# A Fourier layer with a maxout FFN on one core: stores issued by GpSimd, half as many moves for stage Q, half as many loads for the second half of x

## The chip, the cores and the metric

One core of one Trainium2 chip runs the whole program in one launch. The metric is the device time of the launch in microseconds (us). The kernel before took 2103.49 us, the median of 3 runs (2101.82 to 2107.21).

## What is computed

Eight sequences of 3072 tokens with 256 channels go through a Fourier layer: a real FFT along the tokens, a complex 256x256 product with a bias, a soft threshold at 0.01, and the inverse FFT. The 24576 tokens that come out go through a maxout FFN.

```python
x: (8, 3072, 256)   w_r, w_i: (256, 256)   w1, w2, w3: (256, 768)   w_out: (768, 256)

X = np.fft.rfft(x, axis=1)
Yr = Xr @ w_r - Xi @ w_i + b_r
Yi = Xr @ w_i + Xi @ w_r + b_i
Y = soft(Yr) + 1j * soft(Yi)          # soft(v) = sign(v) * max(|v| - 0.01, 0)
y = np.fft.irfft(Y, n=3072, axis=1)   # (8, 3072, 256), as 24576 tokens
h = np.maximum(np.maximum(y @ w1, y @ w2), y @ w3)
out = h @ w_out                       # (24576, 256)
```

## The kernel before

The FFT of length 3072 is done as 96 x 32 by matrix products on TensorE. Most products are of numbers split into two halves of 16 bits (a high and a low part, `split` and `split_later`: ScalarE writes the high part, VectorE the low one) and take three matmuls (`mm3`, lines L175 to L177).

The Fourier layer has these stages for each of the 8 batches, named by the tiles they make:

- **Stage A**, 8 chunks per batch: `load_x` brings a chunk of x (4 of 32 columns), `sum_x` adds and subtracts its two halves on VectorE (from batch 3 on, chunk number `q >= HALF_X`), `split_x` splits it, `stage_a` multiplies by the DFT over 96 into PSUM tile `pa`. ScalarE evicts `pa` to `aq` (L580), and four DMAs per chunk store `aq` to DRAM as `a_d` (L583; in earlier batches one, L596). `load_m` and `largest_m` read the same chunk of x once more (`xm`) for the largest magnitude.
- **Stage B**, 12 steps per batch: `load_a` brings two groups of rows of `a_d` into a tile `ab`, `split_a` splits them in place (ScalarE L635, VectorE L638), and four DMAs on SyncE's queue move the halves across partitions (`ab<-ab`, L643). `stage_b` multiplies by the DFT over 32 into `px` (L732, sixteen matmuls of 64 columns); the results are split again as `tt`.
- **Stage W**, 12 steps: products with the complex weights into `py` (`stage_w1`, `stage_w2`). ScalarE copies the first part to `cs` (L819), VectorE forms `u` from `py` and `cs` (L829), adds the bias and clamps (`soft_threshold`, L777 and L778). `finish_w` splits `u` into `vb` (ScalarE L169, VectorE L170), and eight DMAs on SyncE's queue move it across partitions (`vb<-vb`, L853). Step 11 of each batch is of another kind (`plain`): it has no moves, and GpSimd makes small copies for it (L760 to L769).
- **Stage Q**, once for two steps: `stage_q` begins the inverse transform, `vb` times `qt` into two tiles `pz` (L892); ScalarE evicts to `zs` (L898), and DMAs store `z_d` (L900).
- **Inverse**, 8 chunks per batch: `load_z` brings a chunk of `z_d` as `zq`, `split_z` splits it, `inverse` multiplies into `pi`, split as `yh` and `yl` (ScalarE L169).

The FFN runs all the time from batch 0 on: `up` makes three products per slot into `pu` and the maximum of them (ScalarE copies the first as `c`, L985; VectorE takes the maxima, L988 and L991, the last is `h`, split as `hh`), `down` adds up six slots in `pd`, and ScalarE evicts `pd` to `o` (L1020) three times per chunk, each followed by a store of 128 KB to `out` (L1021).

**Order.** A batch has 48 slots: 8 chunks, each with 6 parts of the FFN's width. Into these slots a list of `events` puts the stages of the later batches: while the FFN of batch b runs, the stages B, W and Q of batch b+1 run at one step per 2.8 slots, and stage A of batch b+2 at one chunk per 5.6 slots. So every batch's stages lie beside an earlier batch's FFN, up to batch 7. The framework then orders each engine's instructions. Each engine issues its own DMAs in its own order: while an engine issues a DMA, what is queued behind on it stands. SyncE (SP) has all loads and all moves; ScalarE (ACT) has the stores of `a`, `z` and `out`; GpSimd (POOL) has a few instructions of step 11 and two loads at the beginning. PSUM has 8 banks: three for `pu`, two for `pd`, and three in turn for `pa`, `px`, `py`, `pz` and `pi` (tag `ff`). Of the buffers that come round in turn, `raw` (tiles `ab` and `vb`) has 8, `aq` and `zs` 2, `o` 3.

Of the kernel before, what the change touches and what calls it, by code (L numbers as in the profile page):

```python
# [9 lines left out]
F32 = mybir.dt.float32  # L10
# [15 lines left out]
def dft_tables():  # L26

    n, n1n, n2n = 3072, 96, 32
    n1, n2, tp = np.arange(n1n), np.arange(n2n), 2 * np.pi
    fa, ga = np.zeros((n1n, 96)), np.zeros((96, n2n, n1n))
    for m in range(94):  # L40
        k1, c = 1 + m // 2, m % 2
        ph = tp * ((k1 * n1) % n1n) / n1n
        fa[:, m] = np.cos(ph) if c == 0 else -np.sin(ph)
        ph = tp * ((k1 * (32 * n1[None, :] + n2[:, None])) % n) / n
        ga[m] = (2.0 / n) * (np.cos(ph) if c == 0 else -np.sin(ph))
    alt = (-1.0) ** n1
    fa[:, 94], ga[94] = 1.0, 1.0 / n
    fa[:, 95], ga[95] = alt, alt[None, :] / n
    sg = np.where(n2 >= 16, -1.0, 1.0)

    def forward(k1):
        ang = tp * ((n2[:, None] * (k1 + 96 * n2[None, :])) % n) / n
        co, si = np.cos(ang), np.sin(ang)
        b = np.zeros((2, 32, 2, 32))
        b[0, :, 0], b[1, :, 0] = co, si
        b[0, :, 1], b[1, :, 1] = -si * sg, co * sg
        return b.reshape(64, 64)

    ang = tp * ((n2[:, None] * n2[None, :]) % 32) / 32
    co, si = np.cos(ang), np.sin(ang)  # L60
    q = np.zeros((2, 32, 2, 32))
    q[0, :, 0], q[1, :, 0] = co, -si * sg[:, None]
    q[0, :, 1], q[1, :, 1] = si, co * sg[:, None]
    bs, qs = np.zeros((2, 32, 2, 32)), np.zeros((2, 32, 2, 32))
    alt = (-1.0) ** n2
    bs[0, :, 0, 0], bs[0, :, 1, 0] = 1.0, alt
    qs[0, 0, 0, :], qs[1, 0, 0, :] = 1.0, alt
    for f in range(1, 32):
        c, k = (0, 96 * f) if f < 16 else (1, 48 + 96 * (f - 16))
        ph = tp * ((k * n2) % n) / n  # L70
        bs[c, :, 0, f], bs[c, :, 1, f] = np.cos(ph), -np.sin(ph)
        qs[0, f, c, :], qs[1, f, c, :] = 2 * np.cos(ph), -2 * np.sin(ph)
    z = np.zeros((64, 64))
    q, bs, qs = (v.reshape(64, 64) for v in (q, bs, qs))
    order = np.arange(128).reshape(2, 2, 32).transpose(1, 0, 2).ravel()
    blocks = [forward(k1) for k1 in range(1, 48)] + [bs]
    mb = [np.block([[blocks[i], z], [z, blocks[i + 1]]])[:, order] for i in range(0, 48, 2)]
    mq = [np.block([[u, z], [z, v]])[order] for u, v in ((q, q), (q, qs))]
    even, odd = (np.pad(fa[0:48, np.arange(96) % 4 // 2 == i], ((0, 16), (0, 16))) for i in (1, 0))
    tiled = np.block([[q, even], [q, odd]])  # L80

    def halves(v, scale):
        v = v * 2.0**scale
        hi = v.astype(np.float16)
        return np.ascontiguousarray(np.stack([hi, (v - hi).astype(np.float16)], 1))

    ga = ga[np.arange(96).reshape(24, 2, 2).transpose(1, 0, 2).ravel()]
    return (
        fa.astype(np.float32),
        halves(ga, SG),  # L90
        halves(np.stack([np.concatenate([v, v]) for v in blocks], 1), SB),
        np.ascontiguousarray(np.stack(mq + mb + [tiled], 1)).astype(np.float32),
        np.eye(128, dtype=np.float32),
    )
# [3 lines left out]
def fourier_maxout_kernel(  # L98
    ctx: ExitStack, tc: tile.TileContext, x, w_r, w_i, b_r, b_i, w1, w2, w3, w_out, fa, ga, mb, mq, ident, out
):  # L100
    nc = tc.nc
    NB, S, D = x.shape
    FF = w1.shape[1]
    P = 128
    N1, N2 = 96, 32
    KD = D // P
    NF = FF // P
    NQ = 4
# [9 lines left out]
    fft = ctx.enter_context(tc.tile_pool(name="fft", bufs=2))  # L118
# [4 lines left out]
    st = {}  # L123
# [87 lines left out]
    def raw_tile(name):  # L211
        return ffn.tile([P, 1536], F32, name=name, tag="raw", bufs=8)
# [257 lines left out]
    def load_x(q):  # L470
        b, q4 = divmod(q, NCH)
        xv = x[b].rearrange("(n1 n2) d -> n1 n2 d", n2=N2)[:, q4 * NQ:(q4 + 1) * NQ, :]
        with tc.issue_after(st["ld"].ins) if q >= EARLY else nullcontext():
            if 2 <= q < NCH or NCH + 2 <= q < EARLY:
                xq = raw_tile("xr")[0:N1, 0:NQ * D]
            else:
                xq = fft.tile([P, NQ * D], F32, name="xq", bufs=2)
                if q >= HALF_X:
                    second = [
                        fft.tile([P, 2, D], F32, name="x2", tag=tag, bufs=3) for tag in ("vl", "vh")  # L480
                    ]
                    xn = xq.rearrange("p (n d) -> p n d", n=NQ)
                    for r, n in ((0, 64), (64, 48)):
                        nc.sync.dma_start(out=xn[r:r + n], in_=xv[0:n])
                    for i, t in enumerate(second):
                        for r, n in ((0, 48), (48, 64)):
                            nc.sync.dma_start(out=t[r:r + n], in_=xv[96 - n:96, 2 * i:2 * i + 2])
                    st["x", q] = xq, second
                    return
                xq = xq[0:N1]  # L490
            nc.sync.dma_start(out=xq.rearrange("p (n d) -> p n d", n=NQ), in_=xv)
            pairs = [xq[:, i * 2 * D:(i + 1) * 2 * D] for i in range(2)]
        st["x", q] = pairs
# [29 lines left out]
        )  # L523

    def sum_x(q):
        xq, second = st.pop(("x", q))
        with in_turn():
            for i, t in enumerate(second):
                half = xq[0:112, i * 512:i * 512 + 512]
                nc.vector.scalar_tensor_tensor(  # L530
                    out=half, in0=t[0:112].rearrange("p n d -> p (n d)"), scalar=sign[0:112], in1=half,
                    op0=ALU.mult, op1=ALU.add,
                )
        st["x", q] = xq
# [28 lines left out]
    def stage_a(q):  # L563
        b, q4 = divmod(q, NCH)
        if q >= HALF_X:
            xt = st.pop(("xs", q))
            pa = [ff_tile("pa") for _ in range(2)]
            aq = fft.tile([P, NQ * D], F32, name="aq", bufs=2)
            for t, i in ((0, 0), (0, 1), (1, 0)):
                for r in range(2):  # L570
                    rows = slice(64 * r, 64 * r + 48)
                    for h in range(2):
                        st["mm"] = nc.tensor.matmul(
                            pa[r][64 * h:64 * h + 64], ft[rows, t], xt[rows, i, h],
                            start=t == i, stop=t == 1,
                        )
            av = batch(b, "a").rearrange("(k e c) n d -> e k c (n d)", e=2, c=2)
            for r in range(2):
                o = aq[:, 512 * r:512 * r + 512]
                nc.scalar.activation(out=o, in_=pa[r], func=AF.Copy, scale=1.0 / (X_SCALE * F_SCALE))  # L580
                for h in range(2):
                    n = q4 * NQ * D + h * 512
                    nc.scalar.dma_start(out=av[1 - r, :, :, n:n + 512], in_=o[64 * h:64 * h + 48])  # L583
            return
        aq = first_quads[q] if q < EARLY else quad_tile("aq")
        for i, xp in enumerate(st.pop(("xs", q))):
          with tc.issue_after(st["gate"]) if EARLY <= q < NATIVE else nullcontext():
# [5 lines left out]
            nc.scalar.activation(  # L593
                out=aq[:, i * 512:i * 512 + 512], in_=pa[0:96], func=AF.Copy
            )
        (nc.scalar if b else nc.gpsimd).dma_start(  # L596
            out=batch(b, "a")[:, q4 * NQ:(q4 + 1) * NQ, :], in_=aq.rearrange("p (n d) -> p n d", n=NQ)
        )
        if NCH <= q < HALF_X and q4 == NCH - 1:
# [119 lines left out]
    def stage_b(k):  # L719
# [5 lines left out]
        if plain(k):  # L725
            pv = px.rearrange("p (h j c q m) -> p h c j q m", h=KD, j=2, c=2, q=2)
        else:
            pv = px.rearrange("p (h c j q m) -> p h c j q m", h=KD, c=2, j=2, q=2)
        for g in range(4):
            for h in range(KD):  # L730
                for i in range(2):
# [105 lines left out]
    def finish_w(k):  # L837
# [3 lines left out]
        if b:  # L841
# [4 lines left out]
            split_later(v[:, 0], v[:, 1], u, st[b, "sv"][0])  # L846

            def move():
                for q in range(2):
                    for j in range(2):  # L850
                        for c in range(2):
                            row = 64 * q + 32 * c
                            nc.sync.dma_start(  # L853
                                out=moved[row:row + 32, kb % 2, :, j],
                                in_=v[64 * j + 32 * q:64 * j + 32 * q + 32, :, c],
                            )

            if not plain(k):
                later(move)
# [6 lines left out]
    def stage_q(k):  # L866
# [17 lines left out]
        elif kb % 2 == 1 or kb == NJP - 2:  # L884
# [11 lines left out]
            for q in range(2):  # L896
                zs = fft.tile([P, 2, D], F32, name="zs")
                nc.scalar.activation(out=zs[:, 0:n], in_=pz[q], func=AF.Copy, scale=st[b, "sv"][1])  # L898
                zv = z_rows(b, q).rearrange("(g j) p d -> (j p) g d", j=2)
                nc.scalar.dma_start(out=zv[:, kb + 1 - n:kb + 1], in_=zs[:, 0:n])  # L900
        if kb == NJP - 1:
            low, add = st["lim", "u"]
            e = exponent_of(st.pop((b, "u")), "u", 23, 0xFF, low)
# [97 lines left out]
    def down(b, c, f, hh):  # L1001
# [10 lines left out]
        if f == NF - 1:  # L1012
            for t in range(3):
# [4 lines left out]
                    )  # L1018
                else:
                    nc.scalar.activation(out=o, in_=pd[t], func=AF.Copy, scale=st[b, "su"][1])  # L1020
                (nc.sync if end and t < 2 else nc.scalar).dma_start(out=out_v[b, c, t], in_=o)  # L1021

    nc.sync.dma_start(out=fr, in_=fa)
    split(fh, fl, fr)
# [188 lines left out]
```

## Time and profile before

| | |
|---|---|
| median of 3 runs | 2103.49 us |
| the profiled execution | 2100.16 us, of which the span 2098.3 us |
| TensorE (PE), busy | 2014.0 us, 96% |
| weight loads (PEld) | 1378.7 us, 66% |
| VectorE (DVE) | 1469.5 us, 70% |
| ScalarE (ACT) | 1034.8 us, 49% |
| GpSimd (POOL) | 21.6 us, 1% |
| mean granted clock of TensorE | 0.991 |

Busy time counts computing instructions alone; the time in which an engine issues DMAs is not in it, and the views show it apart (ACTq, SPq). The span is the time from the first to the last instruction of the profiled execution. Weight loads overlap the matmuls. The granted clock is what the throttle gave, as a share of full speed (1.2 and 2.4 GHz are its two levels, 0.5 and 1 here).

### The profile page before, as it was taken

How to read it: one execution, taken by the hardware profiler on the slowest of the kernel's cores; microseconds unless marked ns; L12 is line 12 of the kernel's file. 1: busy time of each engine (PE TensorE's matmuls, PEld its weight loads, DVE VectorE, ACT ScalarE, POOL GpSimd, SP SyncE). 2: the span in 40 equal slices, each digit the busy share in tenths (PEclk: the TensorE clock that was granted, in tenths of full speed). 3: DMA queues.
4: the chain of work that ended last, by engine and by line, in shares of the span. 5: the costliest groups of instructions: out<-in, count | busy, mean ns of one | idle time of the engine just before them, and what ended most of it. 6: DMA issues, size and time to landing. Idle time of an engine off the chain costs nothing.

```text
span 2098.3 us, 42001 instructions
## 1 busy us (share of the span) xinstructions
PE 2014.0 (96%) x16335; PEld 1378.7 (66%) x16335; DVE 1469.5 (70%) x2809; ACT 1034.8 (49%) x2060; POOL 21.6 (1%) x75
## 2 busy tenths in 40 slices
PE   9989999999899999999999999999999999999999
PEld 5656666666566666666656666666666677766666
DVE  3778887787767877678775777667776567765444
ACT  5745554545444554455544545445554445543333
POOL 0000000000000000000000000000000000000000
PEclk9999999999999999999999999999999999999999
DMA  8745553455433554444444444434443223321110
GB/s 293 214 121 144 149 137 99 129 137 150 121 114 109 140 149 113 134 113 128 136 115 128 115 131 133 126 109 112 129 121 95 69 71 106 87 63 39 31 31 24
DMA packets 227989, 244.67 MB, mean 117 GB/s; under 512 B 30638, under 2 KB 189102, under 8 KB 227694
## 3 DMA queue, kind: packets, MB, share of 16 engines
q1 hardware_dynamic: 161486, 166.46, 30.3%
q10 hardware_dynamic: 65280, 72.12, 10.6%
q0 software_dynamic: 1024, 3.41, 0.5%
q8 instruction: 129, 2.11, 0.4%
q14 instruction: 70, 0.57, 0.1%
HBM read 124.16 MB, written 75.50 MB: 95 GB/s over the span
## 4 chain that ended last, share of the span: by engine, by line
PE 62%; DVE 13%; DMA 10%; ACT 6%; issue 4%; ACTq 3%; SPq 2%; DVEq 0%; POOL 0%; POOLq 0%
PE pu L175 13%; PE pu L176 12%; PE pu L177 12%; PE pd L177 4%; PE pd L176 4%; PE pd L175 4%; DMA ab<-ab 2%; PE py L177 2%; PE py L175 2%; PE py L176 2%; DMA a_d<-aq 2%; PE px L732 1%; DVE c L988 1%; DMA zq<-z_d 1%; DVE h L991 1%
## 5 line engine op out<-in xcount | busy, mean ns | idle before, releaser
L175 PE MATMUL pu<-yh,wuh 128*128 128x384 f16 x2304 | 756.5, 328 | 11.6 <-ACT c L985 9.9
L176 PE MATMUL pu<-yl,wuh 128*128 128x384 f16 x2304 | 755.8, 328 | 0.0
L177 PE MATMUL pu<-yh,wul 128*128 128x384 f16 x2304 | 755.7, 328 | 0.0
L169 ACT ACTIVATE hh<-h 128x384 f16<-128x384 f32 x384 | 199.9, 521 | 451.3 <-DVE h L991 411.8
L988 DVE TENSOR_TENSOR c<-pu,c 128x384 f32<-128x384 f32 x384 | 212.4, 553 | 278.1 <-ACT c L985 175.0
L170 DVE SCALAR_TENSOR_TENSOR hh<-h,hh 128x384 f16<-128x384 f32 x384 | 214.1, 558 | 166.2 <-ACT hh L169 164.3
L177 PEld LDWEIGHTS <-wul 128*128 128x128 f16 x2304 | 226.6, 98 | 151.0 <-issue 3.9
L175 PE MATMUL pd<-woh,hh 128*128 128x256 f16 x1152 | 314.2, 273 | 10.2 <-ACT o L1020 9.7
L175 PEld LDWEIGHTS <-wuh 128*128 128x128 f16 x2304 | 226.4, 98 | 144.2 <-issue 33.8
L176 PE MATMUL pd<-wol,hh 128*128 128x256 f16 x1152 | 314.3, 273 | 0.0
L177 PE MATMUL pd<-woh,hh 128*128 128x256 f16 x1152 | 313.9, 273 | 0.0
L176 PEld LDWEIGHTS <-wuh 128*128 128x128 f16 x2304 | 226.7, 98 | 132.5 <-issue 21.1
L985 ACT ACTIVATE c<-pu 128x384 f32<-128x384 f32 x384 | 187.1, 487 | 180.3 <-PE pu L177 127.8
L991 DVE TENSOR_TENSOR h<-pu,c 128x384 f32<-128x384 f32 x384 | 212.0, 552 | 44.6 <-PE pu L177 38.7
L176 PEld LDWEIGHTS <-hh 128*128 128x128 f16 x1152 | 112.8, 98 | 46.8 <-issue 13.9
L175 PE MATMUL py<-wch,tt 128*128 128x256 f16 x504 | 137.4, 273 | 1.2 <-ACT cs L819 1.2
L177 PE MATMUL py<-wch,tt 128*128 128x256 f16 x504 | 137.3, 272 | 0.0
L176 PE MATMUL py<-wcl,tt 128*128 128x256 f16 x504 | 137.3, 272 | 0.0
L175 PEld LDWEIGHTS <-hh 128*128 128x128 f16 x1152 | 112.8, 98 | 33.6 <-issue 0.5
L1020 ACT ACTIVATE o<-pd,s1u 128x256 f32<-128x256 f32 x191 | 83.0, 469 | 83.7 <-PE pd L177 31.6
L177 PEld LDWEIGHTS <-hh 128*128 128x128 f16 x1152 | 112.8, 98 | 14.2 <-DVE hh L170 0.5
L169 ACT ACTIVATE vb<-u,s0v 128x512 f16<-128x512 f32 x84 | 60.6, 721 | 68.3 <-DVE u L778 35.2
(222 smaller groups left out, 2602.1 us busy)
## 6 DMA issues: line engine op xcount, KB each, us to landing
out_dram<-o ACTq DMA_DIRECT2D x190, 128.0 KB
zq<-z_d SPq DMA_DIRECT2D x63, 384.0 KB
ab<-a_d SPq DMA_DIRECT2D x84, 256.0 KB
ab<-ab SPq DMA_DIRECT2D x336, 64.0 KB
vb<-vb SPq DMA_DIRECT2D x616, 32.0 KB
z_d<-zs ACTq DMA_DIRECT2D x70, 256.0 KB
xm<-in_x_dram SPq DMA_DIRECT2D x40, 384.0 KB
a_d<-aq ACTq DMA_DIRECT2D x160, 96.0 KB
```

Of the source, the lines that this page charges most:

```text
L169: nc.scalar.activation(out=hi, in_=src, func=AF.Copy, scale=scale)
L170: later(lambda: low(nc.vector.scalar_tensor_tensor(out=lo, in0=src, scalar=scale, in1=h, op0=ALU.mult, op1=ALU.subtract)))
L175: nc.tensor.matmul(o, lh, rh, start=start, stop=False, **kw)
L176: nc.tensor.matmul(o, lh, rl, start=False, stop=False, **kw)
L177: st["mm"] = nc.tensor.matmul(o, ll, rh, start=False, stop=stop, **kw)
L732: nc.tensor.matmul(pv[:, h, :, g // 2, g % 2], ah[:, g // 2, g % 2, h * P:(h + 1) * P], mb_sb[:, i, 4 * kb + g].rearrange("p (c m) -> p c ...
L985: st["act"] = nc.scalar.activation(out=c1, in_=p, func=AF.Copy)
L988: st["dve"] = nc.vector.tensor_tensor(out=c1, in0=p, in1=c1, op=ALU.max)
L991: st["dve"] = nc.vector.tensor_tensor(out=h32, in0=p, in1=st["c1"], op=ALU.max)
L1020: nc.scalar.activation(out=o, in_=pd[t], func=AF.Copy, scale=st[b, "su"][1])
```

## The change

Three things are changed; the arithmetic is the same.

1. The stores of `a` (all of them), of `out` (all but the last chunk's) and of `z` where two steps are stored together (70 of 84) are issued by GpSimd. Before, ScalarE issued them (the `a` of batch 0 excepted).
2. The rows of `vb` after its moves are interleaved: the table `qt` gets its rows in another order (`mixed`), stage B writes `px` with the columns in the order of that table (neighbours in `m` lie two apart in PSUM), and the eight moves of 32 rows become four of 64 rows, from and to every second partition.
3. The second half of a chunk of x, before two tiles `vl` and `vh` with two loads each, is one tile of the `raw` ring with two loads.

```diff
+    mixed = q.reshape(2, 32, 64).transpose(1, 0, 2).reshape(64, 64)
-    tiled = np.block([[q, even], [q, odd]])
+    tiled = np.block([[mixed, even], [mixed, odd]])
...
 load_x:
-                    second = [
-                        fft.tile([P, 2, D], F32, name="x2", tag=tag, bufs=3) for tag in ("vl", "vh")
-                    ]
+                    x2 = raw_tile("x2")[:, 0:NQ * D]
...
-                    for i, t in enumerate(second):
-                        for r, n in ((0, 48), (48, 64)):
-                            nc.sync.dma_start(out=t[r:r + n], in_=xv[96 - n:96, 2 * i:2 * i + 2])
+                    xn = x2.rearrange("p (n d) -> p n d", n=NQ)
+                    for r, n in ((0, 48), (48, 64)):
+                        nc.sync.dma_start(out=xn[r:r + n], in_=xv[96 - n:96])
...
 stage_a:
-                    nc.scalar.dma_start(out=av[1 - r, :, :, n:n + 512], in_=o[64 * h:64 * h + 48])
+                    nc.gpsimd.dma_start(out=av[1 - r, :, :, n:n + 512], in_=o[64 * h:64 * h + 48])
...
-        (nc.scalar if b else nc.gpsimd).dma_start(
+        nc.gpsimd.dma_start(
...
 stage_b:
-            pv = px.rearrange("p (h c j q m) -> p h c j q m", h=KD, c=2, j=2, q=2)
+            pv = px.rearrange("p (h c q m j) -> p h c j q m", h=KD, c=2, j=2, q=2)
...
 finish_w:
             def move():
-                for q in range(2):
-                    for j in range(2):
-                        for c in range(2):
-                            row = 64 * q + 32 * c
-                            nc.sync.dma_start(
-                                out=moved[row:row + 32, kb % 2, :, j],
-                                in_=v[64 * j + 32 * q:64 * j + 32 * q + 32, :, c],
-                            )
+                for j in range(2):
+                    for c in range(2):
+                        nc.sync.dma_start(out=moved[c::2, kb % 2, :, j], in_=v[j::2, :, c])
...
 stage_q:
-                nc.scalar.dma_start(out=zv[:, kb + 1 - n:kb + 1], in_=zs[:, 0:n])
+                queue = nc.gpsimd if n == 2 else nc.scalar
+                queue.dma_start(out=zv[:, kb + 1 - n:kb + 1], in_=zs[:, 0:n])
...
 down:
-                (nc.sync if end and t < 2 else nc.scalar).dma_start(out=out_v[b, c, t], in_=o)
+                q = nc.gpsimd if not end else nc.sync if t < 2 else nc.scalar
+                q.dma_start(out=out_v[b, c, t], in_=o)
```

How the instructions then stand: each row is a line, an operation, its tiles (out<-in) and shape; x4 is four in a row. Lines are those of each kernel's own file. First ScalarE at the place that the trace of before has at about 1031 us (`xhl` and `hh` are split tiles of stage A and of the FFN); before:

```order
L169 ACTIVATE xhl<-xq,xx 112x512 x2
L819 ACTIVATE cs<-py,s1x 128x256
L1020 ACTIVATE o<-pd,s1u 128x256 x2
L1021 DMA out_dram<-o 32x4x256
L169 ACTIVATE hh<-h_13597 128x384
L1021 DMA out_dram<-o 32x4x256
L1020 ACTIVATE o<-pd,s1u 128x256
L1021 DMA out_dram<-o 32x4x256
L985 ACTIVATE c_13647<-pu 128x384
L580 ACTIVATE aq<-pa 128x512 x2
L583 DMA a_d<-aq 24x2x512 x4
L898 ACTIVATE zs<-pz,s1v 128x512 x2
```

The same engine and place in the changed kernel:

```order
L170 ACTIVATE xhl<-xq,xx 112x512 x2
L818 ACTIVATE cs<-py,s1x 128x256
L1015 ACTIVATE o<-pd,s1u 128x256 x2
L170 ACTIVATE hh<-h_13375 128x384
L1015 ACTIVATE o<-pd,s1u 128x256
L980 ACTIVATE c_13425<-pu 128x384
L170 ACTIVATE vb<-u,s0v 128x512
L579 ACTIVATE aq<-pa 128x512 x2
L892 ACTIVATE zs<-pz,s1v 128x512 x2
```

The stores are gone from ScalarE, and the split of `u` into `vb` has come ahead of the eviction of `pa` into `aq`.

SyncE at the place that the trace of before has at about 1303 us (`zq` is a chunk of the inverse, `xm` and `x` are chunks of stage A); before:

```order
L942 DMA zq<-z_d 96x1024
L487 DMA x_14325<-in_x_dram 48x512
L643 DMA ab<-ab 64x2x256 x2
L853 DMA vb<-vb 32x2x256 x8
L643 DMA ab<-ab 64x2x256 x2
L508 DMA xm<-in_x_dram 96x1024
L487 DMA x_14325<-in_x_dram 64x512
```

The same chunk in the changed kernel:

```order
L850 DMA vb<-vb 64x2x256 x4
L623 DMA ab<-a_d 128x2x256
L937 DMA zq<-z_d 96x1024
L507 DMA xm<-in_x_dram 96x1024
L642 DMA ab<-ab 64x2x256 x4
L850 DMA vb<-vb 64x2x256 x4
```

The moves of `vb` no longer stand between the moves of one `ab`; they have come ahead of the load of `zq`, a load of `ab` has come between, and the loads of this chunk's second half of x come later.

GpSimd, which has next to nothing to issue before, has this in the middle of a batch of the changed kernel:

```order
L582 DMA a_d<-aq 24x2x512 x4
L1017 DMA out_dram<-o 32x4x256 x3
L582 DMA a_d<-aq 24x2x512 x4
L895 DMA z_d<-zs 128x2x256 x2
L1017 DMA out_dram<-o 32x4x256 x3
```

The stores of the three kinds now stand in one queue, in the order in which they were on ScalarE.

## Rows read from the trace of the kernel before

**Rows 1.** The table of stretches: the stretch and its length in us; then, for PE, PEld, DVE, ACT and POOL, the busy time (and number of instructions); then the mean granted clock, the mean busy share of the DMA engines, and GB/s. Three long stretches.

```profile
100.00:300.00 200.00, 187.40 (x1476) 125.53 (x1474) 162.52 (x307) 109.35 (x216) 0.00 (x0) 0.98 0.52 141
300.00:1650.00 1350.00, 1288.12 (x10873) 879.24 (x10873) 982.44 (x1869) 670.41 (x1351) 12.74 (x48) 0.99 0.44 122
1700.00:2000.00 300.00, 300.00 (x2483) 211.17 (x2482) 193.58 (x349) 135.29 (x272) 1.84 (x8) 1.00 0.24 65
```

**Rows 2.** The same table, two stretches of 100 us.

```profile
1300.00:1400.00 100.00, 93.21 (x770) 62.75 (x769) 69.43 (x130) 46.02 (x92) 1.96 (x8) 0.98 0.41 112
1700.00:1800.00 100.00, 100.00 (x882) 71.48 (x881) 76.87 (x137) 53.25 (x108) 0.00 (x0) 1.00 0.38 99
```

**Rows 3.** The table of waits, PE's, from 300 to 1650 us: who waited, for what; then us in all, how many, and the longest.

```profile
PE pz L892 <- ACT aq L580: 22.9, 20, 3.2
PE px L732 <- DMA ab<-ab: 15.4, 13, 2.4
PE pu L175 <- ACT c L985: 9.2, 12, 2.2
PE pd L175 <- ACT o L1020: 9.0, 10, 1.7
PE pi L175 <- ACT zs L898: 1.5, 1, 1.5
PE pz L892 <- DMA vb<-vb: 1.0, 2, 0.6
```

**Rows 4.** The table of stretches again, windows around the places where the granted clock falls between 300 and 1650 us: the first, the longest and the last of eight.

```profile
303.00:308.00 5.00, 5.00 (x41) 3.02 (x38) 2.06 (x4) 1.81 (x5) 0.00 (x0) 0.71 0.79 239
...
999.00:1007.00 8.00, 6.90 (x44) 3.48 (x44) 1.69 (x4) 3.40 (x7) 0.00 (x0) 0.59 0.54 138
...
1518.00:1523.00 5.00, 5.00 (x41) 2.48 (x35) 0.29 (x1) 1.48 (x3) 0.00 (x0) 0.70 0.58 146
```

**Rows 5.** The timeline of PE at about 1000 and 1312 us: start, duration in us, line, operation, tiles and shape, how many in a row, and in brackets the idle time before and what ended it.

```profile
1000.10 1.49 PE L892 MATMUL pz<-vb,zeros 64*64 64x512 f16 x9 [3.24 <-ACT aq L580]
...
1005.34 0.75 PE L732 MATMUL px<-mb_all,ab 128*128 128x64 f16 x16
...
1006.42 0.33 PE L175 MATMUL pu<-yh,wuh 128*128 128x384 f16 x1
1006.58 0.33 PE L176 MATMUL pu<-yl,wuh 128*128 128x384 f16 x1
...
1312.55 0.28 PE L732 MATMUL px<-mb_all,ab 128*128 128x64 f16 x4 [2.40 <-DMA ab<-ab]
```

**Rows 6.** The timeline of ACT, its DMA issues (ACTq) among it, at about 813, 1000 and 1032 us.

```profile
813.26 0.49 ACT L985 ACTIVATE c<-pu 128x384 f32<-128x384 f32 x1 [5.42 <-DMA a_d<-aq]
...
992.75 2.17 ACTq L1021 DMA_DIRECT2D out_dram<-o  x2
...
999.48 1.06 ACT L580 ACTIVATE aq<-pa 128x512 f32<-128x512 f32 x2
1000.08 3.45 ACTq L583 DMA_DIRECT2D a_d<-aq  x4
...
1031.87 1.09 ACT L580 ACTIVATE aq<-pa 128x512 f32<-128x512 f32 x2 [0.77 <-PE pa L573]
```

**Rows 7.** The timeline of DVE at about 995, 1032 and 1305 us.

```profile
995.47 0.75 DVE L829 SCALAR_TENSOR_TENSOR u<-py,s1x,cs 128x512 f32<-128x512 f32 x1 [3.30 <-ACT cs L819]
...
1032.15 0.68 DVE L778 TENSOR_TENSOR u<-u,t 128x512 f32<-128x512 f32 x1
...
1304.84 0.68 DVE L638 SCALAR_TENSOR_TENSOR ab<-ab 128x512 f16<-128x512 f32 x1
```

**Rows 8.** The timeline of SP's DMA issues at about 1303 to 1312 us.

```profile
1302.86 1.25 SPq L643 DMA_DIRECT2D ab<-ab  x2
1304.20 6.02 SPq L853 DMA_DIRECT2D vb<-vb  x8
1310.32 1.31 SPq L643 DMA_DIRECT2D ab<-ab  x2
```

**Rows 9.** DMA issues by line, over the whole span: how many, then the shortest, median and longest in ns, and when the first and the last started (us); behind the semicolon, where shapes would stand, a dash and the count.

```profile
L583 ACTq DMA_DIRECT2D a_d<-aq x160: 740/752/2315, 393.0 to 1646.5; - x160
L1021 ACTq DMA_DIRECT2D out_dram<-o x190: 546/570/2090, 151.0 to 2094.5; - x190
L900 ACTq DMA_DIRECT2D z_d<-zs x84: 338/378/1053, 221.9 to 1866.3; - x84
L853 SPq DMA_DIRECT2D vb<-vb x616: 585/596/2106, 199.6 to 1856.8; - x154
L643 SPq DMA_DIRECT2D ab<-ab x336: 590/622/1990, 163.9 to 1834.8; - x168
```

**Rows 10.** The timeline of POOL: a load that it issues at 87 us, and two negations of step 11.

```profile
87.55 0.59 POOL L1117 DMA_DIRECT2D bias_ri<-in_b_r_dram  x1
...
317.73 0.40 POOL L760 TENSOR_SCALAR tt<-tt 128x256 f16<-128x256 f16 x1 [228.97 <-DVE c L988]
319.00 1.30 POOL L760 TENSOR_SCALAR tt<-tt 128x256 f16<-128x256 f16 x1 [0.21 <-DVE tt L170]
```

**Rows 11.** Groups of instructions of ACT: line, operation, tiles and shape, how many; busy us in all and mean ns of one; then the idle time before them and what ended it.

```profile
L985 ACT ACTIVATE c<-pu 128x384 f32<-128x384 f32 x384 | 187.1, 487 | 180.3 <-PE pu L177 127.8 <-DMA a_d<-aq 29.2 <-PE px L732 6.1
...
L169 ACT ACTIVATE yh<-pi 128x384 f16<-128x384 f32 x128 | 61.7, 487 | 49.2 <-PE pi L177 48.7
```

More of the change, by code (lines that the diff above doesn't have):

```diff
@@ L484, in load_x @@
                         nc.sync.dma_start(out=xn[r:r + n], in_=xv[0:n])
-                    for i, t in enumerate(second):
-                        for r, n in ((0, 48), (48, 64)):
-                            nc.sync.dma_start(out=t[r:r + n], in_=xv[96 - n:96, 2 * i:2 * i + 2])
-                    st["x", q] = xq, second
+                    xn = x2.rearrange("p (n d) -> p n d", n=NQ)
+                    for r, n in ((0, 48), (48, 64)):
+                        nc.sync.dma_start(out=xn[r:r + n], in_=xv[96 - n:96])
+                    st["x", q] = xq, x2
                     return
@@ L525, in sum_x @@
     def sum_x(q):
-        xq, second = st.pop(("x", q))
+        xq, x2 = st.pop(("x", q))
         with in_turn():
-            for i, t in enumerate(second):
-                half = xq[0:112, i * 512:i * 512 + 512]
+            for i in range(2):
+                half, other = (t[0:112, i * 512:i * 512 + 512] for t in (xq, x2))
                 nc.vector.scalar_tensor_tensor(
-                    out=half, in0=t[0:112].rearrange("p n d -> p (n d)"), scalar=sign[0:112], in1=half,
+                    out=half, in0=other, scalar=sign[0:112], in1=half,
                     op0=ALU.mult, op1=ALU.add,
```

## The prediction

> **What bounds the kernel now.** I began with the table of stretches. TensorE is the bound almost everywhere, and the question is only where it stands still. Between 300 and 1650 us it is busy for 1288.12 of 1350 us, so it idles for 61.9 us; between 100 and 300 us it idles for 12.6 us; between 1700 and 2000 us it does not idle at all [rows 1]. The two 100 us stretches set side by side are the key to the case: at 1300 to 1400 us TensorE is busy for 93.21 us, at 1700 to 1800 us for 100.00 us, although VectorE has more to do in the second (76.87 us against 69.43 us) and ScalarE too (53.25 against 46.02) [rows 2]. In the second stretch the last batch is still in its stages B, W and Q, with their stores on ScalarE's queue and their moves on SyncE's; what has ended (at 1646.5 us, the last of its stores [rows 9]) is stage A, with its loads of x, its sums and its four stores per chunk. So the waits belong to the meeting of stage A with the rest, not to a want of VectorE or ScalarE time.
>
> Next I read who TensorE waits for between 300 and 1650 us [rows 3]: the eviction of `pa` (22.9 us in 20 waits), the moves of `ab` (15.4 in 13), the copies of `c` and `o` (9.2 and 9.0), one eviction of `zs` (1.5). Then the granted clock: in eight places the clock falls to its half level shortly after one of the longer of these waits. In windows around the eight the mean clock is between 0.59 and 0.75; time lost is the window's length times what is missing to 1, 1.45 us in the first, 3.28 in the longest, 1.50 in the last, 13.4 us for all eight [rows 4].
>
> Last I followed two places in the timeline. At 1000 us: ScalarE's queue issues two stores of `out` for 2.17 us from 992.75; the copy `cs` behind them is late, and VectorE, which has nothing else to do, waits 3.30 us for it before it can form `u`. ScalarE then takes `vb` (which needs `u`) and only after that `aq`, at 999.48, and TensorE, which needs the bank that `aq` empties, has waited 3.24 us [rows 5 to 7]. Right after, four stores of `a` hold the queue for 3.45 us [rows 6]. At 813 us the same four hold back the copy `c` by 5.42 us [rows 6]. At 1310 us the cause is SyncE: two moves of `ab`, then eight moves of `vb` that take 6.02 us, then the two other moves of `ab`, whose data were ready at 1305.5 but which are issued at 1310.32; TensorE waits 2.40 us for them [rows 5, 7, 8].
>
> **The change, part by part.** *Stores to GpSimd.* An issue takes 752 ns for a store of `a` (160 of them), 570 for `out` (189 of the 190 move), 378 for `z` (70 of the 84 move) [rows 9]: 120 + 108 + 26 = 254 us of ScalarE's queue, of which the path sees what [rows 3] shows. The waits for `c`, `o` and `zs`, 9.2 + 9.0 + 1.5 = 19.7 us, stand right behind such issues; I take 17. The waits for `aq`, 22.9 us, are of two kinds: some stand behind issues (the place at 1000 us, where 2.17 us would go), others behind VectorE's own chain, which stays. I take half, 11.
>
> On GpSimd the same stores should need about 590 ns apiece, which the trace shows for one load of 128 x 1 KB issued there [rows 10]. About 345 fall between 300 and 1650 us (160 of `a`; of `out` 190 from 151.0 to 2094.5 us are 132 in 1350 us; of `z` the 84 are some 56 [rows 9]), one in 3.9 us, so the queue is used to about 15%. What is queued behind them there is the two negations, two copies and four memsets of step 11 (once in each of seven batches); its stage W is placed 3.8 slots (some 20 us) later, which covers six issues (3.5 us). Cost: nothing, and if the cover is gone, at most 3.5 us in each of seven batches, 25 us. The buffers that a late store keeps are used again after about 30 us (`aq`, `zs`, `o`), so a store that lands some us later costs nothing either. The first half of batch 1 and the end keep ScalarE's or SyncE's queue where the change leaves them.
>
> Speaking against it is one overlap in the trace: GpSimd's negation took 1.30 us beside a VectorE instruction, against 0.40 us alone [rows 10]. The Trainium skill (SBUF — State Buffer, section "Who interferes with whom", and its box on the "DVE blocks DMA" trap) says that a VectorE instruction in a two-port mode locks GpSimd out, so that GpSimd cannot write descriptors, and gives 620 ns that become 3100 ns. By that rule the 345 issues would take 1070 us of 1350 (an estimate from that page's figure), which still fits. How much of VectorE's work here is in such a mode no row tells.
>
> *Four moves for eight.* A move of 32 rows takes 596 ns to issue, one of `ab` with 64 rows 622 ns [rows 9]: the issue hardly depends on the rows. Four moves then take 2.5 us and not 4.8 (6.02 at 1310 us), so the `ab` moves behind them start 2.3 to 3.5 us earlier, more than any wait of [rows 3] for `ab` (2.4 at most). Some of these waits have no `vb` ahead. Of 15.4 us I take 12, and 2 more for `pz` waiting for `vb` (1.0 in this stretch; as much again is an estimate for batch 1, whose moves begin before it). That the rows are now interleaved makes stage B write `px` with step 2. No row shows TensorE writing so. Sixteen such matmuls take 0.75 us [rows 5]; the bounds are 0, and half rate, 0.43 us for each of 77 steps, 33 us. I take 0: ScalarE reads a bank with a step for `yh` in the 487 ns that it needs for `c` without one [rows 11].
>
> *Second half of x.* 160 loads become 80 on SyncE, at a similar price each; their buffer now comes from the `raw` ring of eight. In 5.6 slots the ring gives two `ab`, one `vb` and one `x2`, so a buffer comes round after 11 slots, and none is held for more than about 7: no new wait. Gain taken: 0, since 300 to 1650 us has no wait for x.
>
> *Clock and pipeline.* Of the 13.4 us at half clock I take 9: the places at 303, 815, 1054 and 1313 us hang on waits that go (5.9 us), the others on `aq`, of which half goes. Each wait printed is 0.17 us short, since a matmul of 384 columns is shown as 0.33 us while the next starts after 0.16 [rows 5]; for some 35 waits that go, 5 us.
>
> *Order.* ScalarE now takes `vb` right before `aq` at five of eight places in a batch, before at two; so at some 15 places the eviction of `pa` can wait for `u`. At 1031 us `aq` began at 1031.87 and `u` ended at 1032.83 [rows 6, 7]: with `vb` (0.72 us) first, `aq` would begin 1.6 us later, less what `u` gains by the empty queue. Bounds 0 and 1.6 us; I take 0.4, 6 us in all.
>
> Sum: 17 + 11 + 12 + 2 + 9 + 5 - 6 = 50 us. The profiled execution took 2100.16 us, so 2050 like it; the median of the runs before, 2103.49, lies 3.3 above that execution, which makes **2053 us**.
>
> **Rivals.** *All waits go.* Batch 7 runs beside the same stages without a gap [rows 2]. Then 61.9 + 13.4 + 59 x 0.17 = 85 us go: 2018. Against it: stage A's work itself stays, and some waits are VectorE's.
>
> *The eviction of `pa` stays late.* If `u` comes as late as before, the 15 places cost 1.6 us each and the 11 us are not won, with 4 us of clock: 2053 + 18 + 11 + 4 = 2086.
>
> *The moves do not get cheaper.* If one of 64 rows with a partition step of two takes twice as long, the `ab` waits and their clock stay: 2053 + 12 + 2 + 3 = 2070. For it speaks nothing but the new step.
>
> *The waits only change owner.* VectorE is idle for 27% of 300 to 1650 us; if its chain is next at every place, the time stays near 2100. Against it stands [rows 2].
>
> *Step 2 on TensorE's writes* (the slower side). At half rate 33 us, 2086. It decides from 0.65 us a step (50 us over 77); at a quarter of the rate, 1.3 us a step, 100 us, 2153. Against it: ScalarE's strided reads [rows 11].
>
> *GpSimd starved* (slower too, the page's lock in this kernel). The trace's factor, 1.30 over 0.40, would make 1.9 us of 0.59 and changes nothing. It decides from 3.9 us an issue; then `aq`, `zs` and `o` come free late and ScalarE stands: at 4.4 us, 345 x 4.4 - 1350 = 168 us, 2221.
>
> **How the numbers follow.** Chances: forecast 0.52; all go 0.15; eviction late 0.15; moves no cheaper 0.05; change of owner 0.05; step 2 deciding 0.05; GpSimd starved 0.03. What this kernel's measurement can tell from no change is about 0.3%, 6 us. Faster takes the first four, 0.87; the same 0.05; slower 0.08. The range has to leave out no more than 2 in 10: from 2012, below the case of all waits gone, to 2090, above the late eviction; the last three cases, 0.13, stand outside.
>
> **What would show it.** ScalarE's queue without stores of `a` and `out`, and no wait of ScalarE behind them; the four `vb` moves in about 2.5 us; waits of `px` for `ab` under 4 us and those of `pu` and `pd` near 0; fewer than four places at half clock; 16 matmuls of stage B still in 0.75 us; GpSimd's issues under 1 us. Wrong would be: `pz` waiting for `aq` above 23 us (late eviction), stage B at over 1 us, GpSimd busy above a third, or TensorE busy below 96% between 300 and 1650 us with VectorE as the releaser.

## The result and the profile after

The changed kernel takes 2044.35 us (median of 4 runs, 2042.68 to 2045.16) against 2102.68 for the kernel before (now of 4 runs): 0.9717 of it, with a 95% interval of 0.97 to 0.9734. That is 58 us less; 50 were forecast. The profiled execution has a span of 2042.3 us. How close the two numbers lie is in good part luck, as the experiments show.

The table of stretches of the changed kernel, columns as in [rows 1], which these lines answer together with [rows 2]:

```profile
100.00:300.00 200.00, 193.67 (x1506) 131.62 (x1505) 167.66 (x320) 112.38 (x223) 19.95 (x35) 0.98 0.50 142
300.00:1650.00 1350.00, 1339.61 (x11324) 938.57 (x11322) 1032.68 (x1929) 699.57 (x1403) 223.56 (x397) 1.00 0.46 126
1300.00:1400.00 100.00, 100.00 (x813) 69.11 (x812) 69.02 (x144) 48.02 (x97) 16.99 (x34) 1.00 0.39 109
```

From 300 to 1650 us TensorE idles for 10.4 us and not for 61.9, and the mean clock is 1.00. The stretch from 1300 to 1400 us has become for TensorE what 1700 to 1800 us was before. What TensorE still waits for there (the table of waits, as [rows 3]):

```profile
PE pz L886 <- ACT aq L579: 10.1, 15, 1.1
PE pi L178 <- DVE zl L171: 0.2, 1, 0.2
```

Of the six waits in [rows 3] one is left. The idle time that went (51.5 us here, 6.3 between 100 and 300 us), the eight places at half clock (13.4 us; none is left in this stretch) and 43 waits fewer, each printed 0.17 us too short (7.3 us), make 78 us, but the span became only 56.0 us shorter. So something was paid, and TensorE's timeline shows where (the last three lines are another place, used further down):

```profile
1005.15 1.06 PE L731 MATMUL px<-mb_all,ab 128*128 128x64 f16 x16
...
1246.56 0.84 PE L572 MATMUL pa<-xhl,zeros 48*64 48x512 f16 x12
...
1247.23 0.59 PE L886 MATMUL pz<-vb,zeros 64*64 64x512 f16 x3
1248.89 0.83 PE L886 MATMUL pz<-vb,zeros 64*64 64x512 f16 x9 [1.06 <-ACT aq L579]
```

Sixteen matmuls of stage B take 1.06 us, where [rows 5] has 0.75 and the experiment below 0.63. The 0.75 us are not a price at full clock: they lie in the window of 999 to 1007 us, whose mean clock was 0.59 [rows 4]. The DMA issues by line (count, shortest, median and longest in ns, first and last start) answer to [rows 9]:

```profile
L1017 POOL DMA_DIRECT2D out_dram<-o x189: 550/552/615, 152.5 to 2022.3; - x189
...
L582 POOL DMA_DIRECT2D a_d<-aq x160: 577/590/660, 387.8 to 1587.1; - x160
...
L895 POOL DMA_DIRECT2D z_d<-zs x70: 712/750/759, 221.8 to 1798.1; - x70
...
L850 SPq DMA_DIRECT2D vb<-vb x308: 594/607/1488, 199.1 to 1798.1; - x154
```

GpSimd needs 552 to 750 ns for a store (the medians of the three kinds), never over 759, and a move of 64 rows costs SyncE 607 ns, about what one of 32 did (596 [rows 9]).

### The profile page after: what moved, and what is told of

The parts are those of the page before. It is cut to its first block, busy times and chain, and to the rows that moved or that the text cites. A ratio compares the mean times of both kernels' runs of the same rounds, so it can differ in the third digit from the quotient of the medians.

```text
span 2042.3 us, 42196 instructions
## 1 busy us (share of the span) xinstructions
PE 2015.8 (99%) x16335; PEld 1406.8 (69%) x16335; DVE 1487.7 (73%) x2809; ACT 1036.1 (51%) x2060; POOL 282.5 (14%) x510
## 3 DMA queue, kind: packets, MB, share of 16 engines
q0 software_dynamic: 25168, 68.59, 10.1%
## 4 chain that ended last, share of the span: by engine, by line
PE 87%; DVE 3%; DMA 3%; issue 3%; ACT 2%; SPq 1%; POOL 0%; ACTq 0%; DVEq 0%; POOLq 0%
PE pu L176 17%; PE pu L178 17%; PE pu L177 17%; PE pd L178 6%; PE pd L177 6%; PE pd L176 6%; PE px L731 3%; PE py L178 2%; PE py L176 2%; PE py L177 2%; PE pz L886 1%; PE pa L589 1%; PE pi L178 1%; PE pi L176 1%; PE pi L177 1%
## 5 line engine op out<-in xcount | busy, mean ns | idle before, releaser
L1017 POOL DMA_DIRECT2D out_dram<-o x189 | 104.6, 558 | 1054.3 <-ACT o L1015 1048.7
L582 POOL DMA_DIRECT2D a_d<-aq x160 | 93.7, 590 | 309.7 <-ACT aq L579 307.0
```

The lines of the kernel that those rows point to most:

```text
L582: nc.gpsimd.dma_start(out=av[1 - r, :, :, n:n + 512], in_=o[64 * h:64 * h + 48])
L1017: q.dma_start(out=out_v[b, c, t], in_=o)
```

## The experiments

All ran beside the kernel before, whose median was 2100 to 2102 us in each set. The intervals of e3, e4 and e11 leave out 1, but these three differ from the kernel before by about 2% or less. Waits are PE's between 300 and 1650 us, in us. The last column counts, in the program's order on SyncE, the groups of four `ab` moves (84) that have `vb` moves among them.

| run | time, us | ratio to before, 95% interval | `aq` | `ab` | `c` and `o` | groups |
|---|---|---|---|---|---|---|
| before | 2102 | | 22.9 | 15.4 | 18.2 | 19 |
| the changed kernel | 2044.35 | 0.9717 (0.97 to 0.9734) | 10.1 | 0 | 0 | 3 |
| e1: changed, `px` in natural order | 2011.19 | 0.9574 (0.9547 to 0.9601) | 10.7 | 0 | 0 | 3 |
| e2: only the stores | 2012.56 | 0.9575 (0.9549 to 0.9601) | 10.7 | 0 | 0 | 3 |
| e3: only the moves | 2070.72 | 0.9848 (0.9823 to 0.9872) | 13.0 | 1.7 | 7.1 | 18 |
| e4: only x in one tile | 2090.45 | 0.9945 (0.9925 to 0.9965) | 20.9 | 17.9 | 13.1 | 19 |
| e5: moves, `px` natural | 2051.07 | 0.9755 (0.9737 to 0.9774) | 17.7 | 2.8 | 7.6 | 18 |
| e6: only the stores of `a` | 2051.23 | 0.9754 (0.9733 to 0.9775) | 19.5 | 1.1 | 11.0 | 2 |
| e7: stores, 579 copies instead | 2043.54 | 0.9724 (0.9706 to 0.9742) | 20.7 | 0.5 | 4.9 | 2 |
| e8: stores on SyncE | 2052.37 | 0.9769 (0.9744 to 0.9794) | 10.9 | 17.9 | 0 | 2 |
| e9: e1, `aq` ahead of `vb` | 2001.02 | 0.9523 (0.9504 to 0.9543) | 2.6 | 0 | 0 | 3 |
| e10: stores, 928 copies instead | 2052.47 | 0.9771 (0.9749 to 0.9794) | 21.2 | 5.8 | 6.0 | 2 |
| e11: only the stores of `out` | 2060.34 | 0.9808 (0.9785 to 0.983) | 8.0 | 11.7 | 17.3 | 15 |
| e12: moves and x, `px` natural | 2045.12 | 0.973 (0.9707 to 0.9752) | 18.0 | 4.0 | 5.9 | 17 |

**e1, the step of 2 in PSUM.** Stage B writes `px` as before the change, and each move reads 64 neighbouring rows:

```diff
-            pv = px.rearrange("p (h c q m j) -> p h c j q m", h=KD, c=2, j=2, q=2)
+            pv = px.rearrange("p (h c j q m) -> p h c j q m", h=KD, c=2, j=2, q=2)
...
-                        nc.sync.dma_start(out=moved[c::2, kb % 2, :, j], in_=v[j::2, :, c])
+                        nc.sync.dma_start(out=moved[c::2, kb % 2, :, j], in_=v[64 * j:64 * j + 64, :, c])
```

> The changed kernel with one thing undone: stage B writes px in natural order again (step 1), and each of the four moves of vb reads 64 neighbouring rows (64*j on) in place of every second row. Order of instructions and arithmetic are the same. Theory: the step of 2 in PSUM halves TensorE's rate in stage B; sixteen matmuls took 0.866 us from first to next start in the changed kernel and 0.466 us before, so 77 steps x 0.40 us = 31 us come back: 2044 - 31 = 2013 us, and sixteen matmuls take 0.47 us. Rival: the moves need the source rows spread over all partitions; from 64 neighbouring rows they land later (over 4 us, 2.5 us in the changed kernel), pz waits for vb, and of the 31 us at most 10 are won: 2034 us or more. Second rival: TensorE's faster stage B only makes it wait longer for VectorE and ScalarE: idle time from 300 to 1650 us (10 us in the changed kernel) rises to 30 us or more, 2030 us.

It takes 33 us less than the changed kernel. In its PE timeline the sixteen matmuls take 0.63 us:

```profile
987.68 0.63 PE L731 MATMUL px<-mb_all,ab 128*128 128x64 f16 x16
```

1.06 - 0.63 = 0.43 us, times 77 steps = 33 us: the whole difference. TensorE's busy time over the span falls by as much, from 2015.8 to 1981.9 us. From one start to the next a matmul of 64 columns takes 29 ns in natural order and 56 ns with step 2 (medians). The Trainium skill (SBUF — State Buffer, section "Door 1: The DMA port swizzle", note on cachelines) says that PSUM has cachelines of 8 bytes, two fp32 values, and that a non-contiguous pattern in PSUM slows matmuls significantly; the factor of 1.9 here agrees. The rival fell: the moves land after 2.6 us (median), against 2.5 in the changed kernel. The same section of the Trainium skill holds that partitions 0 to 63 reach no more of SBUF's DMA ports than 0 to 31; at 64 KB a move, these 2.6 against 2.5 us show no price for it.

**e2 to e4, each part alone.** The edits are the parts of the diff above.

> The kernel before with the stores of a, out and the z pairs issued by GpSimd, nothing else. Theory (the terms of the prediction): the waits for c, o and zs (19.7 us) go, half of those for aq, with some 5 us of clock and 4 us of spacing: 36 to 42 us less, 2061 to 2067 us; the waits for moves of ab (15.4 us) stay. Rival (the eviction of pa stays late): the waits for aq stay at 20 us or more and the time is 2075 to 2085. Other rival: the stores carry the whole gain and the moves none, 2020 us or less without the cost of step 2.

> The kernel before with the interleaved rows, the four moves and stage B's writes with step 2, nothing else. Theory: the moves win 14 us of waits and some 6 us of clock and spacing, step 2 costs 31 us on TensorE: 2103 - 20 + 31 = 2114 us, slower than before. Rival (step 2 costs what is hidden behind waits, since TensorE stands for ScalarE's queue anyway): 2095 us or less. The forecast of the prediction (step 2 costs nothing) would give 2083.

> The kernel before with the second half of x in one tile of the raw ring and two loads in place of four, nothing else. Theory: no change, 2103 us plus or minus 5; the waits of PE for ab moves stay near 15 us. Rival: 80 issues of about 0.6 us less on SyncE bring the moves of ab forward, the waits for ab fall under 8 us, and the time is 2090 us. Second rival: x2 takes buffers of the raw ring, loads of ab come later, and the time is above 2110.

In all three the theory was missed. e2 is the case of its last rival; e3 has the time of its rival, and e5 tells how far the reason holds; e4 has the time of its first rival but not its sign, since the waits for `ab` stay at 17.9 us, and where its 11 us come from stays open. The stores alone win 89 us, as much as everything together without step 2 (e1): the order of the instructions on TensorE, VectorE and ScalarE is the same in e1 and e2, and so is the time within 1.4 us. So four moves for eight and one tile for x are worth nothing once the stores have left ScalarE, although alone they win 31 us (step 2 and its price included) and 11 us. e2's waits, the same table as [rows 3]:

```profile
PE pz L892 <- ACT aq L580: 10.7, 15, 1.4
PE pi L177 <- DVE zl L170: 0.2, 1, 0.2
```

The waits for `ab` are gone with all eight moves of 32 rows in place. e2's timeline of SP shows how, at the place that answers to [rows 8]:

```profile
1241.82 3.10 SPq L643 DMA_DIRECT2D ab<-ab  x4
...
1248.51 5.14 SPq L853 DMA_DIRECT2D vb<-vb  x8
```

The eight moves still take over 5 us, but they no longer stand between the halves of an `ab`. With the stores gone the framework puts the split into `vb` earlier on ScalarE (2.2 instructions in the mean), and SyncE's order changes with it: 3 of 84 groups have `vb` moves among them where 19 had. TensorE's order changes too, at about 2% of its matmuls. The waits for `ab` go with the last column: 15.4 and 17.9 us at 19 groups, 11.7 at 15, 1.7 to 4.0 at 17 or 18 groups with half as many `vb` moves (e3, e5, e12), about 1 or none at 2 or 3, unless something else holds SyncE (e8) or ScalarE (e10). That is a correlation over runs; no run changed SyncE's order by itself.

**e5, the moves without step 2.**

> The kernel before with four moves of 64 rows for eight of 32 and the interleaved table for stage Q, but with px written in natural order (the moves read 64 neighbouring rows); stores and x as before. Theory: the moves alone win some 60 us of TensorE's waits, of which the kernel with step 2 (2071 us) gave 31 back; without it 2071 - 31 = 2040 us, and sixteen matmuls of stage B take 0.47 us. Rival: with the stores on ScalarE's queue TensorE waits anyway, so a faster stage B only lengthens its waits: 2055 us or more.

Between theory and rival: 20 of the 31 us come back. Where TensorE waits for something else, part of its slower stage B lies in the waits: those for `aq` are 13.0 us in e3 and 17.7 here, in the same order of TensorE, VectorE and ScalarE.

**e6 and e11, the stores of `a` or of `out` alone.**

> The kernel before with the stores of a alone issued by GpSimd; those of out and z stay on ScalarE. All three together gave 2012.6 us. Theory: what counts is how long ScalarE's queue is held at one time, 3.45 us by the four stores of a against 0.6 to 2.2 by those of out; so this part alone wins more than its share of the issue time (120 of 254 us, 42 of the 89 us): 2045 us or less, and PE's waits for aq from 300 to 1650 us fall under 14 us. Rival: the gain goes by the issue time removed: 2059 us plus or minus 6. Second rival: the stores of out, which stand ahead of the copies for the FFN, carry most: 2075 us or more.

> The kernel before with the stores of out alone issued by GpSimd; those of a and z stay on ScalarE. The stores of a alone gave 2051 us, all three 2012.6 us. Theory: the two parts add up, and this one with z is worth 2051 - 2012.6 = 39 us: 2063 to 2068 us. Rival: either part alone removes most of the waits, since a wait needs both queues late: 2050 us or less. Second rival: with the stores of a still in ScalarE's queue nothing is won: 2085 us or more.

The stores of `a` win 51 us and those of `out` 40, together 91 against 89 for all three: these two parts add up, roughly by the issue time removed (120 and 108 us), with somewhat more for `a`. e6 lies between its theory and its first rival, and its waits for `aq` stay over the theory's 14 us; e11 lies 3 us below its theory. What each removes can be read from the costliest waits, e6 first, then e11:

```profile
PE pz L892 <- ACT aq L580: 19.5, 20, 2.4
PE pu L175 <- ACT c L985: 11.0, 5, 2.5
PE pz L892 <- DMA vb<-vb: 1.8, 2, 1.0
PE px L732 <- DMA ab<-ab: 1.1, 3, 0.6
...
```

```profile
PE pu L175 <- ACT c L985: 14.7, 14, 2.7
PE px L732 <- DMA ab<-ab: 11.7, 9, 2.5
PE pz L892 <- ACT aq L580: 8.0, 18, 1.2
PE pd L175 <- ACT o L1020: 2.6, 6, 0.7
...
```

e11's timeline of ACT at 786 us shows the stores of `a` in one piece of 6.16 us, with the copy `c` behind them:

```profile
786.52 6.16 ACTq L583 DMA_DIRECT2D a_d<-aq  x4
792.73 0.49 ACT L985 ACTIVATE c<-pu 128x384 f32<-128x384 f32 x1 [5.75 <-DMA a_d<-aq]
```

With `a` gone from ScalarE the waits for `o` go and those for `ab` all but go, while those for `aq` (19.5 us) and `c` (11.0) stay; with `out` gone the waits for `aq` fall to 8.0 us and those for `c` rise to 14.7. This bears out the first of two places in [rows 6]: at 1000 us stores of `out` stand ahead of `cs` and so of `aq`. At the second, 813 us, stores of `a` stand ahead of `c`, but taking them away does not take away the waits for `c`; of e2, e6 and e11 only e2, where all these stores leave, is without them.

**e7 and e10, ScalarE's time put back.** The stores go through GpSimd, and copies into a tile that nobody reads any more follow on ScalarE (e7: two for each store of `a`, one for each other; e10: three for `a`, two for `out`, one for `z`):

```diff
+    def spend(src):
+        nc.scalar.activation(out=qf.rearrange("p i m -> p (i m)"), in_=src, func=AF.Copy)
...
                     nc.gpsimd.dma_start(out=av[1 - r, :, :, n:n + 512], in_=o[64 * h:64 * h + 48])
+                    for d in range(2):
+                        spend(o[:, 256 * d:256 * d + 256])
```

> The kernel before with the stores on GpSimd as in the run of the stores alone (2012.6 us), and in place of each store that left ScalarE a copy on ScalarE into a tile that nobody reads any more (128 or 48 to 64 rows by 256 columns, about 0.4 us; two of them for each store of a): 579 copies, some 250 us, against 254 us of issues before. The copies' results are not used. VectorE's and TensorE's orders stay those of the run of the stores alone but for a few places. Theory: what the stores cost is ScalarE's time at those places: the time goes back to 2080 us or more, with waits for aq, c and o. Rival: the gain came from the new order of instructions that the framework chose when the stores left, or from the stores going through another DMA queue: 2030 us or less.

> The run of the stores on GpSimd with copies of 256 columns on ScalarE in their place (2043.5 us), with more of them: three for each store of a, two for each of out, one for z, 928 in place of 579. The 579 had added only 137 us to ScalarE's busy time from 300 to 1650 us, since such copies follow each other in about 0.28 us, where the issues that left took some 216 us there. Theory: the gain of the stores is ScalarE's time alone; now about as much time is put back as the issues took, and the time is 2080 us or more. Rival: part of the gain is not ScalarE's time (the order of instructions, or the way through another DMA queue): 2065 us or less.

The page of e10 has ScalarE busy for 285 us more than e2's (1029.8 us), more than the 254 us of issues:

```profile
PE 1994.5 (97%) x16335; PEld 1376.3 (67%) x16335; DVE 1480.2 (72%) x2809; ACT 1314.9 (64%) x2988; POOL 282.3 (14%) x510
```

31 us are lost again in e7, between theory and rival, and 40 of the 89 in e10, the rival's case, with the waits for `aq` near their old size (20.7 and 21.2). So ScalarE's time is a cause, but not shown to be the whole. TensorE's order stays that of e2 but for a few places and only 2 groups have `vb` moves among them, which goes with low waits for `ab` (0.5 and 5.8 us); the rest of SyncE's order is not e2's (in e10 about a fifth of its DMAs stand elsewhere). The copies are no full likeness of the stores either: the framework spreads them between other instructions, where the four stores of `a` stand in one piece (3.45 us in [rows 6], 6.16 in e11).

**e8, the stores on SyncE.** e2 with `nc.sync` for `nc.gpsimd` in the three places.

> The run of the stores alone (2012.6 us), with the same stores issued by SyncE in place of GpSimd; the orders on TensorE, VectorE and ScalarE are the same. Theory: the stores wait for evictions, and on SyncE the loads and the moves of ab and vb stand behind them: px waits for moves of ab again, 15 us or more from 300 to 1650 us, and the time is 2040 us or more. Rival: any queue but ScalarE's will do, since SyncE waits for nothing that TensorE needs soon: 2012 to 2022 us.

As the theory had it, 40 of the 89 us are lost, at the same order on TensorE, VectorE and ScalarE. The two costliest waits, one place of SP's timeline, and PE's behind it:

```profile
PE px L732 <- DMA ab<-ab: 17.9, 14, 4.5
PE pz L892 <- ACT aq L580: 10.9, 15, 1.6
...
```

```profile
1257.38 3.33 SPq L583 DMA_DIRECT2D a_d<-aq  x4
1260.81 0.98 SPq L901 DMA_DIRECT2D z_d<-zs  x2
1261.88 6.01 SPq L853 DMA_DIRECT2D vb<-vb  x8
1267.99 0.53 SPq L943 DMA_DIRECT2D zq<-z_d  x1
1268.62 1.33 SPq L643 DMA_DIRECT2D ab<-ab  x2
...
1270.71 1.24 SPq L643 DMA_DIRECT2D ab<-ab  x2
```

```profile
1275.62 1.05 PE L732 MATMUL px<-mb_all,ab 128*128 128x64 f16 x16 [4.49 <-DMA ab<-ab]
```

Stores of `a` and `z` hold SyncE from 1257.38 to 1261.79 us; the moves of `vb` begin only behind them, and those of `ab` behind `vb`, the last pair at 1270.71. At 1275.62 us TensorE has waited 4.49 us for them, its longest wait. The stores need a queue on which nothing urgent stands behind them; leaving ScalarE is not enough.

**e9, `aq` ahead of `vb`.** Over e1, the split into `vb` is held behind the last eviction of `pa`:

```diff
-                nc.scalar.activation(out=o, in_=pa[r], func=AF.Copy, scale=1.0 / (X_SCALE * F_SCALE))
+                st["evict"] = nc.scalar.activation(
+                    out=o, in_=pa[r], func=AF.Copy, scale=1.0 / (X_SCALE * F_SCALE)
+                )
...
-            split_later(v[:, 0], v[:, 1], u, st[b, "sv"][0])
+            with tc.issue_after(st["evict"].ins) if "evict" in st else nullcontext():
+                split_later(v[:, 0], v[:, 1], u, st[b, "sv"][0])
```

> The changed kernel with px in natural order (2011 us), and the split of u into vb on ScalarE held behind the last eviction of pa, so that aq never stands behind a vb that waits for VectorE's u. In 25 places vb and aq change places; TensorE's order is the same. Theory: the 15 waits for aq (10.7 us from 300 to 1650 us) are this order's price; most of them go, and VectorE's and SyncE's part of vb can bear to come 1 us later: 2001 to 2006 us, waits for aq under 4 us. Rival: the three banks of PSUM that pa and pz share set these waits (four tiles in a row), whatever comes first: waits for aq above 8 us and the time 2009 us or more.

It came out as the theory had it, and it is the best version: 2001.02 us, 43 us below the changed kernel. ScalarE's timeline in the changed kernel, where TensorE waits 1.06 us at 1248.89 (above):

```profile
1247.63 0.72 ACT L170 ACTIVATE vb<-u,s0v 128x512 f16<-128x512 f32 x1 [1.45 <-DVE u L777]
1248.26 1.06 ACT L579 ACTIVATE aq<-pa 128x512 f32<-128x512 f32 x2
```

and in e9 at the same place of the program, then PE's:

```profile
1219.15 1.09 ACT L579 ACTIVATE aq<-pa 128x512 f32<-128x512 f32 x2 [1.25 <-PE pa L572]
1220.12 0.72 ACT L170 ACTIVATE vb<-u,s0v 128x512 f16<-128x512 f32 x1
```

```profile
1219.80 0.83 PE L889 MATMUL pz<-vb,zeros 64*64 64x512 f16 x9 [0.26 <-ACT aq L579]
```

ScalarE stood 1.45 us for VectorE's `u` and then wrote `vb`, and began `aq` at 1248.26 us, although the matmuls into `pa` end at 1247.40 (1246.56 + 0.84); now it empties the bank first, and TensorE's wait falls to 0.26 us.

**e12, all but the stores.**

> The change without its first part and without step 2: four moves, interleaved table, second half of x in one tile, px in natural order, the stores still on ScalarE. The moves alone gave 2051 us, x alone 2090. Theory: the two relieve the same queue (SyncE's), so x adds less than its 11 us: 2043 to 2050 us, and waits for aq, c and o stay above 20 us in all. Rival: with both, SyncE's queue is so early that ScalarE's lateness is covered too: 2030 us or less.

The theory held for the time (2045 us; x adds 6 us to the moves). Without moving the stores 55 us are to be had, with the stores alone 89, with both 90 (e1).

## Why the prediction was right, and where its steps were wrong

The time lay inside the range because two errors met: the waits won nearly twice what was summed up, and stage B gave a third of it back at a price that was put at nothing.

- **Step 2 on TensorE's writes** was the step that failed outright: taken as 0 between bounds of 0 and 33 us, it costs 33 us (e1), the far bound. The prediction's own sign of being wrong, stage B at over 1 us, came (1.06). The 0.75 us that it took as today's price was partly at half clock; at full clock it is 0.63. The reason for 0 was ScalarE's reads of a bank with a step [rows 11]. A read by another engine is no row for a write by TensorE; with no near row the middle of the bounds, or the half rate itself as the likeliest case, would have been the honest value. The rival with this price stood in the text with 2086 us and 0.05, as if all else stayed put.
- **The gain of the waits** was 50 us in the sum and is 89 or 90 without step 2 (e2, e1); the rival "all waits go" had priced it at 85, with a chance of 0.15. Its evidence, [rows 2], was the best in the profile and was given too little weight. Term by term, from 300 to 1650 us: `c`, `o` and `zs` 19.7 us for the 17 taken; `ab` 15.4 for 12; the clock 13.4 for 9; `aq` 12.8 for 11 less 6, and 20 with e9's order.
- **What removes which wait** was counted once where it can be had twice. The waits for `ab` were put down to the eight moves' length, and the four moves alone do take them from 15.4 to 1.7 or 2.8 us (e3, e5). But the stores alone take them away too (e2), it seems by way of the order that the framework then chooses, and beside that the fewer moves add nothing (e1 against e2).
- **Half of the `aq` waits belong to VectorE's chain, which stays:** about half did stay with the stores gone (10.7 us in e2), but not for good. VectorE's chain reaches TensorE there because `vb`, which waits for `u`, stands ahead of `aq`; with `vb` behind, 2.6 of 22.9 us are left (e9). The order's price had the right mechanism, and only its size was low: 6 us in all, where e9 against e1 takes away 8.1 us of these waits and 10 us of the time.
- **x in one tile at 0** agrees with e1 and e2 within the change and was wrong alone (11 us, e4).
- **GpSimd** did as priced: 552 to 750 ns an issue (medians) for the 590 taken. The Trainium skill (SBUF — State Buffer, section "A bandwidth-pool intuition that's wrong (but worth ruling out)") gives about 3100 ns for a DMA issued by GpSimd that overlaps a VectorE copy; nothing of the kind is in 419 stores (longest 759 ns).

What stays open: how the 49 us that e10 did not take back divide between the new order (on SyncE and on the other engines), the unbroken pieces of time that the stores took on ScalarE, and the way through GpSimd's queue. That would need the old order with the stores on GpSimd, or the new one with them on ScalarE, which was not tried. Of the span, 78 us of found time less 33 leave 45 of the 56 us; 11 us I can't place by rows.

## What to carry to other kernels

Where engines issue their own DMAs, price a store by what stands behind it on its queue, and look whether a stretch of the same kernel already runs without waits: here the case that all waits go, as in that stretch, was priced at 85 us, and 89 were won without step 2, while a sum of single waits, each cut down for what might stay, came to 50. A part that wins alone may win nothing beside another that removes the same waits, so measure parts both alone and left out. And when a layout is changed to make DMAs cheaper, let the DMA carry the step: a contiguous write of the matmul and a strided destination of the move did the same for nothing.

## What the runs showed of the hardware

- A matmul that writes 64 fp32 columns to PSUM with a step of 2 takes 56 ns from start to start, and 29 ns without the step, at full clock (the changed kernel and e1).
- A DMA of 64 rows costs its issuer about as much as one of 32 (607 and 596 ns), whether its source rows are every second partition or neighbours (605 ns in e1).
- GpSimd issued a store of 96 KB (24x2x512) in 590 ns where ScalarE took 752 [rows 9], but one of 256 KB (128x2x256) in 750 ns where ScalarE took 378.
